# Sign bits in four matmul passes, V's maximum by DMA, shared idle matmuls and a new order in a fused attention and MoE kernel

## The chip, the core and the metric

The kernel runs on one core of a Trainium2 chip. The metric is the device time of one execution in microseconds (us), lower is better. The core has a matrix engine (TensorE, PE in the profile, with its weight loads as PEld), a vector engine (VectorE, DVE), a scalar engine (ScalarE, ACT), GpSimd (POOL), and SyncE (SP), which here issues every DMA. Each engine runs its own instructions in the order in which they were issued and waits for the others by semaphores. PE writes to PSUM; DVE and ACT read PSUM and SBUF; POOL reads SBUF.

## What is computed

Attention in which a query sees only the keys of its own hash bucket, and behind it a layer that mixes tokens and channels. There are 4 batches, 8 heads, 768 tokens, 64 channels per head and 6 hash bits.

```python
q_bits = (np.einsum('bhsd,dk->bhsk', q, proj) > 0).astype(np.int64)
k_bits = (np.einsum('bhsd,dk->bhsk', k, proj) > 0).astype(np.int64)
...
mask = q_bucket[:, :, :, None] == k_bucket[:, :, None, :]
scores = scale * np.matmul(q, k.transpose(0, 1, 3, 2))
scores = np.where(mask, scores, -1000000000.0)
scores = scores - np.max(scores, axis=-1, keepdims=True)
attn = np.exp(scores)
attn = attn / (np.sum(attn, axis=-1, keepdims=True) + 1e-09)
return np.matmul(attn, v).astype(np.float32)
...
theta = x @ w_theta
cos_t, sin_t = (np.cos(theta), np.sin(theta))
zr = x * cos_t
zi = x * sin_t
yr = np.einsum('ts,bsd->btd', w_tok_r, zr)
yi = np.einsum('ts,bsd->btd', w_tok_i, zi)
y = yr + yi
u = x + y
return (u + np.maximum(u @ w_ch, 0.0)).astype(np.float32)
```

## The kernel before

**Numbers in parts.** Single matmul passes carry fewer bits than fp32, so values are split into a high and a low part and multiplied in several passes. q and k are split by `high` (an ACT copy to a narrower fp32 form, line 643) and `low` (the remainder, line 646, on DVE or POOL) into the tile `hl`.

**Work by pairs of heads.** `prep_qk` and `prep_v` prepare two heads at once, 16 pairs in all. For the sign bits `bits` (line 660) multiplies `hl` by the projection's parts `pst` in two halves of 512 and 256 tokens, each into its own PSUM bank `pb`: three passes for q (high by high, high by low, low by high), three for k, accumulated into the same 64 rows. `sign` (line 668) compares those rows with 0 on DVE and writes `rows`. `first` (line 673) does the same for the very first head straight into qt and kt. `assemble` (line 710) copies `hl` and `rows` by DMA into the operands qt and kt of one head; three sets of these take turns (`SETS`).

**One head.** `maxima` (line 742) computes the scores `sq` once, in nine units, each reduced by DVE (`vmax`, line 768, tile `mc`), transposes the maxima on PE (`pmx`), makes a row of them and writes it into qt by DMA (`put`). `step` (line 812) then computes transposed scores `st`, now with the maximum subtracted in the matmul, exponentiates them on ACT (`pf`, line 846), and multiplies by V in `pv` (line 860), which accumulates `po`. A head has nine chunks of 128 by 512 (six in block 0, three in block 1), a pair 18. In a pair whose number is in `FULL` the fp32 `pf` is multiplied by the whole scaled V (`vw`). In the others `pf` becomes two fp16 parts, p1 (a copy, line 852) and p2 (the remainder, line 858), and three passes follow with V's two parts. `P1` and `P2` name the engines for these parts by step number.

**V's scale.** `prep_v` reduces the absolute maximum of V to one value per partition (`amax`, DVE, line 519), transposes it on PE into PSUM (`am_tr`), reduces it on DVE (`am_row`), multiplies it by ones on PE to bring it to all partitions (`am_all`), and copies it out (`am_out`, line 533). A power of two made of it scales V.

**MoE.** For every batch `moe` (line 915) transposes x in six token tiles (`pt_x`), multiplies by w_theta (`ps_th`), makes cosine and sine (`trig`), the products z in two fp16 parts, multiplies by the token weights (`py`, 36 passes a tile), adds, transposes again (`pt_u`), multiplies by w_ch (`ps_r`) and stores. The weights are prepared during the first pairs: token weights by `prep_wtok` (due times `W0`, `WS`), w_theta and w_ch by `split_weight` (`WTH`, `WC`).

**The order.** Nothing is issued where it is written. Each `op` has a name, a due time (`prio`, in steps; 96 steps in all, six to a pair), the engines it may run on with planned durations, the ops it waits for and the buffer slots it holds. `issue_all` (line 120) simulates the engines with those durations and issues for each engine, when it falls free, the available op with the earliest due time. The constants behind the function (`QK1`, `PV0`, `TH0`, `Y0`, `YS` and others) are those due times. If PE has nothing to do before `FILL`, it issues an idle matmul (`filler`, line 323), planned at 225 ns; each gets a new tile in a free bank of the PSUM pool `m`. That pool has four banks, the pools `mx` and `s` have two each.

Of the kernel before, what the change touches and what calls it, by code (L numbers as in the profile page):

```python
# [32 lines left out]
def lsh_attention_moe_kernel(ctx: ExitStack, tc: tile.TileContext, qk, wt, v, consts, w_theta, w_ch, out):  # L33
# [6 lines left out]
    P = 128  # L40
# [33 lines left out]
    psts = const.tile([P, 2, 2, 96], F32R, name="pst")  # L74
    POOL.memset(psts.bitcast(F32), 0.0)
    pst = {}
    for i, part in enumerate("hl"):
        flat = psts[:, i].rearrange("p a b -> p (a b)")
        pst["q", part], pst["k", part] = flat[:, :64], flat[:, 64:128]
# [12 lines left out]
    WAKE = {"ACT": 45, "DVE": 37, "PE": 58, "POOL": 105, "SP": 40}  # L92
    SHARED = {"qkl", "p1", "p2", "zf", "zh", "zl", "mag", "wlow", "whigh", "wmul", "wl", "vv2", "wtl"}
# [21 lines left out]
    FREE = dict(ft=2, mc=2, hl=1, rows=1, nat=2, wst=2, vv=2, x=2, z0=1, z1=1, xt=2, **BUFS)  # L115
# [3 lines left out]

    def issue_all():  # L120
        left = {}
        rng = random.Random(SEED)
        for i, o in enumerate(ops):
            o.key = (round(o.prio + JIT * rng.random(), 4), i)
            for sl in o.slots:
                left.setdefault(sl, []).append(o)
# [74 lines left out]
        used, seen, warm = {}, 0, False  # L201

# [119 lines left out]

    def filler(idx):
# [42 lines left out]
    def widened(srcs, n, nm, tag, prio, stage="x", by=1.0):  # L366
# [22 lines left out]
        a = op("wload", prio, on("SP", [(450, P * n * 8)] * m, load), slots=[sx, sz])  # L389
# [36 lines left out]
    def prep_wtok(n, prio):  # L426
# [26 lines left out]
        a = op("wload", prio, on("SP", [(450, P * S * 8)], load), slots=sl)  # L453
# [46 lines left out]
    vamax, vinv, vsc = (const.tile([P, B * NP], F32, name=nm) for nm in ("vamax", "vinv", "vsc"))  # L500
    zinv, zsc = (const.tile([P, B], F32, name=nm) for nm in ("zinv", "zsc"))
    vready = {b: [] for b in range(B)}

    def prep_v(b, hp, prio):
        t = {}
        sv, sm_, sa = Slot("vv"), Slot("m"), Slot("m")
# [14 lines left out]
        def am_tr():  # L521
            t["pa"] = bank(sa, [P, 2, P], f"pa_{b}_{hp}")
            PE.transpose(t["pa"][:1, 0], t["am"], ident)

        def am_row():
            t["a1"] = ap_.tile([1, 1], F32, tag="a1" + sa.tag, bufs=1, name=f"a1_{b}_{hp}")
            DVE.tensor_reduce(t["a1"], t["pa"][:1, 0], AX.X, ALU.max)

        def am_all():
            mm(t["pa"][:, 1, :2], t["a1"].to_broadcast([1, P]), ones1, True, True)  # L530

        def am_out():
            DVE.tensor_copy(vamax[:, col], t["pa"][:, 1, :1])
# [92 lines left out]
    def prep_qk(b, hp, G, g):  # L626
# [4 lines left out]
        for i in range(2):  # L631
            def half(i=i):
# [7 lines left out]
                def high():  # L640
                    if "hl" not in t:
                        t["hl"] = ap_.tile([P, 2, 2, S], F32R, tag=sh.tag, bufs=1, name=f"hl_{b}_{hp}")
                    ACT.activation(t["hl"][:, 0, i], u["nat"], AF.Copy)  # L643
# [3 lines left out]

                ld = op("qkload", G + QKL + 0.02 * i, on("SP", [(450, 2 * S * D * 4)], load), slots=[sn])
                hs.append(op("qkh", pr, on("ACT", 735, high), [ld], [sn, sh]))
# [5 lines left out]
        for lo, n_ in ((0, 512), (512, S - 512)):  # L655
            def signs(lo=lo, n_=n_):
# [580 lines left out]
```

## Time and profile before

| | us |
|---|---|
| median of 3 runs | 829.23 |
| lowest and highest | 828.43, 829.85 |
| profiled execution, its own time | 830.03 |
| span of its trace | 828.2 |
| DMA queue, share of 16 engines | 37.2% |

The profile shows one execution. Busy times are the time in which an engine had an instruction in flight. Matmuls are pipelined, so that one's own duration is longer than its distance to the next; the cost of a run of matmuls is read from the start of the next run. A view by groups lists line, engine, operation, output and inputs, count, busy us and mean ns of one, and then the idle time in front of them with what ended it. The chain of waits follows the work that ended last back from the end. A view by windows gives busy times in stretches, with the instruction count in brackets, and then the granted clock of PE, the share of the DMA engines and GB/s.

### The profile page before, as it was taken

What the parts mean: (1) busy time and instruction counts of PE and PEld (TensorE: products, weight loads), DVE (VectorE), ACT (ScalarE), POOL (GpSimd) and SP (SyncE); (2) the same over time, 40 slices, a digit from 0 to 9 for tenths busy, and PEclk for the clock granted to TensorE, in tenths of its full rate; (3) what the DMA queues carried; (4) which work ended last, traced back from release to release, by engine and by line L of the source; (5) the groups of instructions that cost most, each with busy time, mean ns of one, the idle gap of its engine ahead of it and who ended that gap; (6) DMA issues with size and microseconds to landing.
All of it is one profiled execution on the core that took longest, in us unless ns stands there. A gap on an engine that the chain in (4) does not pass through costs nothing.

```text
span 828.2 us, 17207 instructions
## 1 busy us (share of the span) xinstructions
PE 808.8 (98%) x6644; PEld 569.7 (69%) x6644; DVE 602.8 (73%) x1024; ACT 511.1 (62%) x871; POOL 372.9 (45%) x404
## 2 busy tenths in 40 slices
PE   8999999999999999999999999999999999999997
PEld 2588887676765667878667666678667666676554
DVE  5869989886896957797888766687988666357322
ACT  3366766785993635797987365467985554568100
POOL 2344444773676614684766342352685332113100
PEclk9999999999999999999999999999999999999999
DMA  8466759407016424544243434251333330000001
GB/s 231 99 201 189 223 151 240 123 11 168 18 44 156 121 60 122 127 87 108 69 96 85 112 94 110 57 141 33 93 81 82 76 74 14 15 27 1 13 26 38
DMA packets 33617, 79.00 MB, mean 95 GB/s; under 512 B 6360, under 2 KB 10648, under 8 KB 33536
## 3 DMA queue, kind: packets, MB, share of 16 engines
q1 hardware_dynamic: 33536, 77.91, 37.2%
q8 instruction: 52, 0.85, 0.4%
q14 instruction: 29, 0.24, 0.1%
HBM read 32.54 MB, written 6.29 MB: 47 GB/s over the span
## 4 chain that ended last, share of the span: by engine, by line
PE 87%; DVE 6%; ACT 4%; issue 1%; DMA 1%; SPq 1%; ACTq 0%; DVEq 0%
PE py L82 21%; PE po L82 15%; PE st L82 15%; PE ps_r L82 8%; PE sq L82 8%; PE ps_th L82 7%; PE fill L82 5%; PE pb L82 4%; DVE mc L768 2%; PE pt_u L957 1%; PE pt_x L957 1%; ACT pf L846 1%; PE pa L82 1%; ACT p L852 1%; DVE mc L777 1%
## 5 line engine op out<-in xcount | busy, mean ns | idle before, releaser
L846 ACT ACTIVATE pf<-st 128x512 f32<-128x512 f32 x288 | 167.8, 596 | 134.2 <-PE st L82 126.3
L858 POOL TENSOR_TENSOR p<-pf,p 128x512 f16<-128x512 f32 x135 | 167.5, 1252 | 182.7 <-ACT p L852 119.8
L768 DVE TENSOR_REDUCE mc<-sq 128x1 f32<-128x512 f32 (+1 forms) x288 | 191.5, 683 | 34.1 <-PE sq L82 32.4
L82 PE MATMUL py<-z,wtk 128*128 128x512 f16 x864 | 215.7, 381 | 0.0
L82 PE MATMUL st<-qt,kt 108*128 108x512 f32 (+3 forms) x768 | 195.8, 364 | 2.8 <-ACT pf L846 2.6
L852 ACT ACTIVATE p<-pf 128x512 f16<-128x512 f32 x234 | 140.7, 632 | 9.2 <-PE po L82 7.0
L82 PEld LDWEIGHTS st<-qt,kt 108*128 108x128 f32 (+1 forms) x768 | 119.1, 190 | 20.9 <-ACT pf L846 8.5
L82 PE MATMUL sq<-kt,qt 108*128 108x512 f32 (+1 forms) x384 | 128.9, 393 | 2.7 <-DVE mc L768 1.2
L82 PEld LDWEIGHTS <-wtk 128*128 128x128 f16 x864 | 72.4, 98 | 83.5 <-issue 18.3
L82 PEld LDWEIGHTS <-p 128*128 128x128 f16 x2808 | 106.8, 98 | 31.1 <-issue 14.0
L82 PE MATMUL po<-vv,p 128*128 128x65 f16 (+1 forms) x2808 | 124.5, 193 | 0.4 <-DVE p L858 0.4
L858 DVE TENSOR_TENSOR p<-pf,p 128x512 f16<-128x512 f32 x99 | 87.5, 888 | 35.0 <-ACT p L852 32.9
L82 PEld LDWEIGHTS sq<-kt,qt 108*128 108x128 f32 x384 | 66.7, 190 | 23.0 <-DVE mc L768 5.8
L1046 POOL TENSOR_TENSOR z<-f,z 128x512 f16<-128x512 f32 x34 | 46.4, 1370 | 59.6 <-ACT z L1040 40.3
L82 PE MATMUL ps_r<-wch,h_u 128*128 128x512 f32 x192 | 62.8, 408 | 0.7 <-ACT h_u L962 0.7
L82 PE MATMUL ps_th<-wth,h_x 128*128 128x512 f32 x192 | 62.0, 404 | 0.1
L789 POOL TENSOR_SCALAR fl<-row 6x128 f16<-6x128 f32 x32 | 28.4, 889 | 62.1 <-DVE row L785 44.7
L82 PEld LDWEIGHTS po<-vw,pf 128*128 128x128 f32 x432 | 54.5, 192 | 1.8 <-issue 0.2
L82 PE MATMUL po<-vw,pf 128*128 128x65 f32 x432 | 54.6, 274 | 0.0
L962 ACT ACTIVATE h_u<-pt_u 128x512 fp32r<-128x512 f32 x24 | 14.3, 597 | 64.0 <-PE pt_u L957 63.9
L82 PE MATMUL fill<-idle 128*128 128x512 f16 x121 | 48.0, 404 | 5.5 <-DVE ones L72 1.6
L646 POOL TENSOR_TENSOR hl<-nat,hl 128x768 fp32r<-128x768 f32 x24 | 48.1, 2013 | 10.6 <-ACT hl L643 10.5
(139 smaller groups left out, 1079.7 us busy)
## 6 DMA issues: line engine op xcount, KB each, us to landing
nat<-in_qk_dram SPq DMA_DIRECT2D x32, 384.0 KB
qt<-hl SPq DMA_DIRECT2D x31, 384.0 KB
kt<-hl SPq DMA_DIRECT2D x31, 384.0 KB
wst<-in_wt_dram SPq DMA_DIRECT2D x12, 768.0 KB
vb<-in_v_dram SPq DMA_DIRECT2D x16, 384.0 KB
out_dram<-x SPq DMA_DIRECT2D x24, 256.0 KB
qt<-hl SPq DMA_DIRECT2D x62, 96.0 KB
kt<-hl SPq DMA_DIRECT2D x62, 96.0 KB
```

The costliest lines, as they stand in the source:

```text
L82: PE.matmul(out_, l, r, start=start, stop=stop, skip_group_check=True)
L646: return lambda: eng.tensor_tensor(t["hl"][:, 1, i], u["nat"], t["hl"][:, 0, i].bitcast(F32), ALU.subtract)
L768: DVE.tensor_reduce(col()[:, cs], u["sq"], AX.X, ALU.max)
L777: DVE.tensor_tensor(t["mc"][:, :T], t["mc"][:, :T], t["mc"][:, T:], ALU.max)
L789: POOL.tensor_scalar(t["fl"], t["row"].bitcast(F32), -BIG / 4, PSC, ALU.is_lt, ALU.mult)
L846: ACT.activation(wide("pf", spf, F32), u["st"], AF.Exp, scale=1.0 / math.sqrt(D))
L852: ACT.activation(o_, u["pf"], AF.Copy)
L858: return lambda: eng.tensor_tensor(wide("p2", sp2, F16), u["pf"], u["p1"], ALU.subtract)
L957: PE.transpose(u["pt"][:, c], src()[:, c * P : (c + 1) * P], ident)
L962: ACT.activation(u["hi"], u["pt"], AF.Copy)
L1046: return lambda: eng.tensor_tensor(t["z"][r, 1][:, tt], u["f"], t["z"][r, 0][:, tt], ALU.subtract)
```

## The change

- **Sign bits.** The projection's high part lies in columns 0 to 63 of a 128-column operand, its remainder (now with the opposite sign) in columns 64 to 127. One pass of the high part of q gives both products, in PSUM rows 0 to 63 and 64 to 127; the low part needs one pass of 64 columns. So two passes for q and two for k. ACT copies rows 64 to 119 to SBUF (`total`), DVE subtracts them from rows 0 to 55 (`plus`), and `sign` compares in SBUF, on DVE or POOL.
- **V's maximum.** The transpose is a DMA of the 128 values into a row (`vrow`), the distribution a DMA of one value to 128 partitions. The PSUM bank that held the two products is not taken; the row is one buffer (`vr`).
- **Idle matmuls.** A filler writes again into the tile of the filler before, as long as that is the newest tile of its bank. Planned at 216 ns.
- **Order.** The planner counts extra time for a wide fp32 pass behind certain ops (`AFTER`, `WIDE`) and prefers, behind these, another op that is due up to `PEN` later. Tails by name count on PE alone. Some planned durations change. The projection may be split on POOL, and the constants are loaded behind the first q and k. In the first pair the high parts may be made on DVE.
- **Constants.** `FULL` loses pair 1. `P1` is ACT and `P2` POOL throughout. Nearly all due times are new.

```diff
-    psts = const.tile([P, 2, 2, 96], F32R, name="pst")
+    psts = const.tile([P, 2, 160], F32R, name="pst")
...
+    flat = psts.rearrange("p a b -> p (a b)")
+    pst = {"q": flat[:, :P], "k": flat[:, P : 2 * P]}
...
+    AFTER = {"pv": 84, "pv4": 30, "mtr": 40, "vall": 40, "xtr": 20}
+    WIDE = {"st", "qmax", "proj", "bits"}
...
+                    if best is not None and o.key[0] > best[0] + PEN:
+                        break
+                    if best is not None and o.name in WIDE:
+                        continue
                     if can(o):
-                        best, pick = o.key, o
-                        break
+                        best, pick = best or o.key, o
+                        if e != "PE" or o.name not in WIDE or before not in AFTER:
+                            break
...
-                lat = TAILS.get(o.name, TAIL_[e])
+                lat = TAILS.get(o.name, TAIL_[e]) if e == "PE" else TAIL_[e]
                 if e == "PE":
+                    if o.name in WIDE:
+                        dur += AFTER.get(before, 0)
+                    before = o.name
...
-        return op("fill", 0, on("PE", 225, lambda: mm(bank(sl, [P, 512], "fill"), idle_[:, :P], idle_, True, True)))
+        def go():
+            if sl.tag not in spare or spare[sl.tag] is not newest.get(sl.tag):
+                spare[sl.tag] = bank(sl, [P, 512], "fill")
+            mm(spare[sl.tag], idle_[:, :P], idle_, True, True)
+
+        return op("fill", 0, on("PE", 216, go))
...
+            h_, l_ = psts[:, :, : 2 * NM], psts[:, :, 64 : 64 + 2 * NM]
...
+            eng.tensor_tensor(l_, h_.bitcast(F32), pjs, ALU.subtract)
...
+    cload = op("consts", QKL + 0.03, on("SP", [(600, 0)], load_consts))
+    proj_ready = op("pst", PST, {"POOL": (1500, split_proj(POOL)), "DVE": (1100, split_proj(DVE))}, [cload])
...
         def am_tr():
-            t["pa"] = bank(sa, [P, 2, P], f"pa_{b}_{hp}")
-            PE.transpose(t["pa"][:1, 0], t["am"], ident)
+            dma(vrow, t["am"])
 
         def am_row():
-            t["a1"] = ap_.tile([1, 1], F32, tag="a1" + sa.tag, bufs=1, name=f"a1_{b}_{hp}")
-            DVE.tensor_reduce(t["a1"], t["pa"][:1, 0], AX.X, ALU.max)
+            DVE.tensor_reduce(vone, vrow, AX.X, ALU.max)
 
         def am_all():
-            mm(t["pa"][:, 1, :2], t["a1"].to_broadcast([1, P]), ones1, True, True)
-
-        def am_out():
-            DVE.tensor_copy(vamax[:, col], t["pa"][:, 1, :1])
+            dma(vamax[:, col], vone.to_broadcast([1, P]))
...
                 def bits():
                     u["pb"] = bank(sm_, [P, 512], f"pb_{b}_{hp}_{lo}")
-                    n = 0
-                    for i, nm in enumerate("qk"):
-                        for a_, c in (("h", 0), ("h", 1), ("l", 0)):
-                            mm(u["pb"][:64, :n_], pst[nm, a_], t["hl"][:, c, i, lo : lo + n_], n == 0, n == 5)
-                            n += 1
+                    cols = slice(lo, lo + n_)
+                    mm(u["pb"][:, :n_], pst["q"], t["hl"][:, 0, 0, cols], True, False)
+                    mm(u["pb"][:, :n_], pst["k"], t["hl"][:, 0, 1, cols], False, False)
+                    mm(u["pb"][:64, :n_], pst["q"][:, :64], t["hl"][:, 1, 0, cols], False, False)
+                    mm(u["pb"][:64, :n_], pst["k"][:, :64], t["hl"][:, 1, 1, cols], False, True)
...
+                    ACT.activation(u["r"].bitcast(F32), u["pb"][64:120, :n_], AF.Copy)
+
+                def plus():
+                    DVE.tensor_tensor(u["r"].bitcast(F32), u["pb"][:56, :n_], u["r"].bitcast(F32), ALU.subtract)
+
+                def sign(eng):
+                    return lambda: eng.tensor_scalar(u["r"], u["r"].bitcast(F32), affs[:56, 0:1], affs[:56, 1:2], ALU.is_ge, ALU.mult)
...
-FULL = [0, 1, 2]
+FULL = [0, 2]
...
-P1 = [[0, 12, ['ACT', 'DVE']], [12, 999, ['ACT']]]
-P2 = [[0, 999, ['POOL', 'DVE']]]
+P1 = [[0, 999, ['ACT']]]
+P2 = [[0, 999, ['POOL']]]
...
-Y0_3 = 16.204
-YS_3 = 7.658
-Y1_3 = 3.219
+Y0_3 = 32.886
+YS_3 = 18.321
+Y1_3 = 0.085
...
-QK1 = -5.44
-PV0 = -4.578
-W0 = 2.347
-WS = 1.758
+PEN = 0.282
+QK1 = -3.942
+PV0 = -4.358
+W0 = 1.598
+WS = 2.439
```

More of the change, by code (lines that the diff above doesn't have):

```diff
@@ L201, in issue_all @@
         used, seen, warm = {}, 0, False
+        before = None
         def pace(t, dur, part):
@@ L452, in prep_wtok @@
         sl = [sw_]
[L453 removed]
+        a = op("wload", prio, on("SP", [(350, P * S * 8)], load), slots=sl)
         b_ = op("wlow", prio, on("DVE", 80 + 400, low), [a], sl)
@@ L500, in lsh_attention_moe_kernel @@
     vamax, vinv, vsc = (const.tile([P, B * NP], F32, name=nm) for nm in ("vamax", "vinv", "vsc"))
+    vrow = const.tile([1, P], F32, name="vrow")
+    vone = const.tile([1, 1], F32, name="vone")
     zinv, zsc = (const.tile([P, B], F32, name=nm) for nm in ("zinv", "zsc"))
@@ L638, in load, with high, go @@
                     dma(u["nat"], qk[b, hp, :, i])
[L640 to L643, printed above, removed]
+                def high(e):
+                    def go():
+                        if "hl" not in t:
+                            t["hl"] = ap_.tile([P, 2, 2, S], F32R, tag=sh.tag, bufs=1, name=f"hl_{b}_{hp}")
+                        if e == "ACT":
+                            ACT.activation(t["hl"][:, 0, i], u["nat"], AF.Copy)
+                        else:
+                            DVE.tensor_copy(t["hl"][:, 0, i], u["nat"])
+                    return go
                 def low(eng):
                     return lambda: eng.tensor_tensor(t["hl"][:, 1, i], u["nat"], t["hl"][:, 0, i].bitcast(F32), ALU.subtract)
-                ld = op("qkload", G + QKL + 0.02 * i, on("SP", [(450, 2 * S * D * 4)], load), slots=[sn])
-                hs.append(op("qkh", pr, on("ACT", 735, high), [ld], [sn, sh]))
+                ld = op("qkload", G + QKL + 0.02 * i, on("SP", [(330, 2 * S * D * 4)], load), slots=[sn])
+                hs.append(op("qkh", pr, {"ACT": (735, high("ACT")), "DVE": (475, high("DVE"))} if g == 0 else on("ACT", 735, high("ACT")), [ld], [sn, sh]))
                 ls.append(op("qkl", pr, {"DVE": (870, low(DVE)), "POOL": (1750, low(POOL))}, [hs[-1]], [sn, sh]))
@@ L675, in first @@
                         DVE.tensor_scalar(
-                            dst[MR : MR + NM, 0, lo : lo + n_], u["pb"][r0 : r0 + NM, :n_], affs[r0 : r0 + NM, 0:1], affs[r0 : r0 + NM, 1:2], ALU.is_ge, ALU.mult
+                            dst[MR : MR + NM, 0, lo : lo + n_], u["r"].bitcast(F32)[r0 : r0 + NM], affs[r0 : r0 + NM, 0:1], affs[r0 : r0 + NM, 1:2], ALU.is_ge, ALU.mult
                         )
-                b1 = op("bits", G + at("QK1", b), on("PE", 10 + 1388 * n_ / 512, bits), hs + ls + [proj_ready], [sm_, sh])
+                pr1 = G + at("QK1", b)
+                b1 = op("bits", pr1, on("PE", 10 + 925 * n_ / 512, bits), hs + ls + [proj_ready], [sm_, sh])
+                b1 = op("btot", pr1, on("ACT", 60 + 420 * n_ / 512, total), [b1], [sm_, sr])
+                b1 = op("bplus", pr1, on("DVE", 70 + 540 * n_ / 512, plus), [b1], [sm_, sr])
+                rest = []
                 if g == 0:
-                    t.setdefault("direct", []).append(op("sign0", G + at("QK1", b) - 0.01, on("DVE", 2 * (230 + 560 * n_ / 512), first), [b1], [sm_]))
-                fs.append(op("sign", G + at("QK1", b), on("DVE", 190 + 540 * n_ / 512, sign), [b1], [sm_, sr]))
+                    rest = [op("sign0", pr1 - 0.01, on("DVE", 2 * (70 + 280 * n_ / 512), first), [b1], [sr])]
+                    t.setdefault("direct", []).extend(rest)
+                fs.append(op("sign", pr1, {"DVE": (65 + 272 * n_ / 512, sign(DVE)), "POOL": (90 + 1030 * n_ / 512, sign(POOL))}, [b1] + rest, [sr]))
             signs()
@@ L1132 @@
 WIN = {"m": 3, "tmp": 3}
-MX0 = -4.222
-MX1 = 0.485
+MX0 = -3.92
+MX1 = 0.367
 PIECES = [{1: (0, 3)}, {0: (0, 2), 1: (2, 3)}]
-PF = 0.229
-KA = 1.914
-KB = 1.297
-KV = 0.471
-KN = 2.21
-AB = -1.043
-WTH = 17.154
-WTS = -3.096
-WC = 28.626
-WCS = 1.32
-P1 = [[0, 12, ['ACT', 'DVE']], [12, 999, ['ACT']]]
-P2 = [[0, 999, ['POOL', 'DVE']]]
+PF = 0.656
+KA = 2.074
+KB = 1.097
+KV = 0.9
+KN = 1.554
+AB = -1.588
+WTH = 17.112
+WTS = 0.063
+WC = 25.356
+WCS = 4.365
+P1 = [[0, 999, ['ACT']]]
+P2 = [[0, 999, ['POOL']]]
 GR = 2
-GR1 = 2
+GR1 = 0
 GROUPS = [[(0, 3), (3, 6)], [(0, 4), (4, 6)], [(0, 2), (2, 4), (4, 6)]]
-JIT = 0
-SEED = 162248
-TH0_3 = 4.023
-TH1_3 = 0.304
-Y0_3 = 16.204
-YS_3 = 7.658
-Y1_3 = 3.219
-MX0_0 = -2.545
-MX1_0 = -0.458
-AS0_0 = -5.127
-PV0_0 = -3.986
-QK0_0 = -2.659
-QK1_0 = -8.282
-HOLD = 0.312
-FILL = 190000
-TH0_0 = 0.49
-TH1_0 = 0.849
-Y0_0 = 10.381
-Y1_0 = 1.107
-YS_0 = 5.176
-AHEAD = 1.931
-QKL = -8.066
-QK0 = -3.777
-QK1 = -5.44
-AS0 = -1.124
-PV0 = -4.578
-LV0 = -3.999
-W0 = 2.347
-WS = 1.758
-TH0 = 0.512
-TH1 = 0.818
-Y0 = 10.167
-YS = 6.472
-Y1 = 2.716
+TH0_3 = 4.252
+TH1_3 = 0.07
+Y0_3 = 32.886
+YS_3 = 18.321
+Y1_3 = 0.085
+MX0_0 = -2.536
+MX1_0 = 0.04
+AS0_0 = -4.728
+PV0_0 = -6.631
+QK0_0 = -6.273
+QK1_0 = -10.464
+HOLD = 0.177
+FILL = 190000
+TH0_0 = 0.566
+TH1_0 = 0.25
+Y0_0 = 10.85
+Y1_0 = 2.254
+YS_0 = 8.488
+PEN = 0.282
+AHEAD = 1.948
+PST = -12.621
+QKL = -8.174
+QK0 = -2.283
+QK1 = -3.942
+AS0 = -4.062
+PV0 = -4.358
+LV0 = -3.808
+W0 = 1.598
+WS = 2.439
+TH0 = 1.365
+TH1 = 0.38
+Y0 = 9.202
+YS = 6.317
+Y1 = 2.708
 _INS = ["v", "moe_w_theta", "moe_w_ch"]
```

53 lines of the change are left out of this document (26 added, 27 removed).

## The prediction

> **What bounds the kernel now.** I read the page first: busy times, then the shares of the chain of work that ended last.
>
> ```profile
> PE 808.8 (98%) x6644; PEld 569.7 (69%) x6644; DVE 602.8 (73%) x1024; ACT 511.1 (62%) x871; POOL 372.9 (45%) x404
> PE 87%; DVE 6%; ACT 4%; issue 1%; DMA 1%; SPq 1%; ACTq 0%; DVEq 0%
> PE py L82 21%; PE po L82 15%; PE st L82 15%; PE ps_r L82 8%; PE sq L82 8%; PE ps_th L82 7%; PE fill L82 5%; PE pb L82 4%; DVE mc L768 2%; PE pt_u L957 1%; PE pt_x L957 1%; ACT pf L846 1%; PE pa L82 1%; ACT p L852 1%; DVE mc L777 1%
> ```
>
> PE is busy 98% of the span and 87% of the chain, so a pass taken from PE should come off the end. But 5% of the chain is `fill`, the idle matmul that computes nothing: there PE was waiting for others. Next I asked for engine busy times by stage, and then the same for the fills alone (first number the length, then PE busy; in the first fence PEld, DVE, ACT and POOL follow, in brackets the instructions).
>
> ```profile
> 33.00:66.00 33.00, 32.78 (x227) 27.52 (x226) 25.23 (x49) 19.68 (x34) 13.53 (x16) 1.00 0.74 206
> 66.00:101.00 35.00, 34.22 (x253) 30.11 (x252) 32.31 (x64) 24.64 (x42) 16.72 (x17) 1.00 0.71 197
> 142.00:166.00 24.00, 23.20 (x212) 14.94 (x212) 21.22 (x44) 19.17 (x37) 17.16 (x20) 1.00 0.52 129
> 166.00:187.00 21.00, 20.16 (x228) 14.74 (x225) 18.27 (x32) 17.52 (x31) 16.02 (x14) 1.00 0.07 21
> ```
> ```profile
> 0.00:33.00 33.00, 23.33 (x56) 1.00 0.55 158
> 33.00:142.00 109.00, 6.70 (x18) 1.00 0.73 200
> 142.00:187.00 45.00, 12.46 (x33) 1.00 0.31 78
> 187.00:220.00 33.00, 5.53 (x15) 1.00 0.46 102
> ```
>
> So there are three regimes. Up to 33 us PE waits for the first head. From 33 to 142 us, where pairs 0 to 2 multiply whole fp32 weights (`FULL`), and after 220 us, PE is the bound. From 142 to 187 us, with split fp16 weights and no MoE matmuls yet, fills take 12.46 of 45 us: there DVE, ACT and POOL set the pace.
>
> **The change, part by part.** The sum is made against the profiled execution, 830.0 us for a span of 828.2; the median of the three runs, 829.2, lies 0.8 below it.
>
> *Sign bits.* The timeline of PE gives each run's start, so its cost is the next start less its own.
>
> ```profile
> 306.31 1.58 PE L82 MATMUL pb<-hl,pst 128*64 128x512 f32 x6
> 307.72 0.63 PE L82 MATMUL ps_r<-wch,h_u 128*128 128x512 f32 x2
> 310.52 0.86 PE L82 MATMUL pb<-hl,pst 128*64 128x256 f32 x6
> 311.23 0.54 PE L82 MATMUL po<-vv,p 128*128 128x65 f16 x12
> 311.61 0.63 PE L957 MATMUL pt_u<-ident,x 128*128 128x128 f32 x4
> 312.47 1.20 PE L82 MATMUL st<-qt,kt 108*128 108x256 f32 x6
> 313.60 0.38 PE L82 MATMUL pa<-ones,a 1*128 1x2 f32 x2
> 313.90 0.73 PE L82 MATMUL ps_r<-wch,h_u 128*128 128x512 f32 x2
> ```
>
> Six 512-column passes take 1.41 us (0.235 each), six of 256 columns 0.71 (0.118 each): 2.12 us a pair. Four of each take 1.41. Fifteen pairs behind the first: 15 x 0.71 = **10.6 us less**. Two of the four passes now load 128 weight columns instead of 64. The groups of weight loads, and a run of 256-column scores that loads 128 columns for each pass:
>
> ```profile
> L82 PEld LDWEIGHTS pb<-hl,pst 128*64 128x64 f32 x192 | 25.3, 140 | 11.5 <-issue 1.2 <-ACT qt L693 0.6 <-DVE x L1074 0.3
> L82 PEld LDWEIGHTS st<-qt,kt 108*128 108x128 f32 (+1 forms) x768 | 119.1, 190 | 20.9 <-ACT pf L846 8.5 <-issue 0.2
> 169.24 0.63 PE L82 MATMUL st<-qt,kt 108*128 108x256 f32 x4
> 169.71 0.54 PE L82 MATMUL po<-vv,p 128*128 128x65 f16 x12
> ```
>
> The wide load shows 190 ns against 140, but four passes with it start within 0.47 us, 0.118 each: nothing shows, and I add nothing. The Trainium skill ("TensorE: Matmul & The Clock Gate", LDWEIGHTS) says that a weight load's time goes with its columns alone, which the 140 and 190 ns follow in direction. If its extra 50 ns were not hidden on the four wide loads of a pair, 16 pairs would give back 3.2 us; the row at 169.24 speaks against it, and the sum goes without.
>
> The result is now two halves to be subtracted: an ACT copy from PSUM, a DVE subtraction, and a comparison that reads SBUF, on DVE or POOL.
>
> ```profile
> L671 DVE TENSOR_SCALAR rows<-pb,cst 56x512 fp32r<-56x512 f32 (+1 forms) x32 | 20.8, 665 | 7.7 <-PE pb L82 7.7
> L852 ACT ACTIVATE p<-pf 128x512 f16<-128x512 f32 x234 | 140.7, 632 | 9.2 <-PE po L82 7.0
> L858 POOL TENSOR_TENSOR p<-pf,p 128x512 f16<-128x512 f32 x135 | 167.5, 1252 | 182.7 <-ACT p L852 119.8
> L858 DVE TENSOR_TENSOR p<-pf,p 128x512 f16<-128x512 f32 x99 | 87.5, 888 | 35.0 <-ACT p L852 32.9
> L646 POOL TENSOR_TENSOR hl<-nat,hl 128x768 fp32r<-128x768 f32 x24 | 48.1, 2013 | 10.6 <-ACT hl L643 10.5
> ```
>
> By these, 32 halves add at most 32 x 0.63 = 20 us to ACT (511 busy), and to DVE nothing or about what L671 takes, 21 us. Their cover is that a pair's bits are due some 4 steps ahead of their use (`QK1`). Without it each half would be late by an ACT and a DVE step, about 1.3 us: 0 taken, +20 us (15 pairs) the far end.
>
> *V's maximum.* The two `ones` passes take 0.30 us (313.60 to 313.90), the transpose before them 0.03 to 0.1: 15 x 0.35 = **5.2 us less**. In exchange 32 DMAs of 512 bytes are queued on SP. The nearest priced transfer is the row of maxima (with the score that waits for it):
>
> ```profile
> 29.42 0.71 SPq L792 DMA_DIRECT2D qt<-row  x1
> 33.22 0.63 PE L82 MATMUL st<-qt,kt 108*128 108x512 f32 x2
> ```
>
> Each holds SP for about 0.7 us, 22 us in all, and lands within 3.8 us. SP now waits for DVE's `am` and `vone`; behind it stand the assembly of qt and kt and the stores. DVE waits at `vone` for a landing, and `vmax`, which frees PE's score banks, stands behind it. V is asked for 4 steps ahead (`PV0`), over 25 us, as 96 steps take some 700 us, so I take 0; 16 x 2 waits of 0.3 us would be +10, the far end. Freeing one `m` bank of PSUM can help by as little.
>
> *FULL without pair 1.* Its 18 chunks take 8 fp32 records each now, and would take 12 fp16 passes. The fp32 chunk stands in the chain in order of time:
>
> ```profile
> 45.02 0.84 PE po L82 x8
> ```
>
> 0.84 less 0.38 (311.23 to 311.61) is 0.46; x 18 = **8.3 us less** on PE in a stage that PE bounds. It adds 18 x 0.63 = 11 us to ACT and 18 x 1.25 = 23 us to POOL there. Pair 1 ran from 66 to 101 us, where ACT is busy 24.6 and POOL 16.7 of 35: with it they come to 36 and 39, over the stage. They fit only with what lies beside it: 33 to 66 us has 13 us of ACT and 19 of POOL idle, and the preparation of the token weights, which uses both, is spread out (`WS` 1.76 to 2.44). With 0 and 2 whole and 1 and 3 split, PE-heavy and POOL-heavy pairs alternate, so I count the gain in full and keep the doubt for the rivals.
>
> *P1, P2.* All narrow copies go to ACT, all remainders to POOL. The 99 on DVE become 99 x 1.25 = 124 us of POOL; with pair 1 it has about 373 + 124 + 23 = 520 us: under the end, but see the second rival. DVE loses 88 us, where it was the fullest next to PE (21.2 of 24 us).
>
> *Idle matmuls and the start.*
>
> ```profile
> 6.66 0.96 DVE L646 TENSOR_TENSOR hl<-nat,hl 128x768 fp32r<-128x768 f32 x1 [0.21 <-ACT hl L643]
> 9.36 4.11 PE L82 MATMUL pb<-hl,pst 128*64 128x512 f32 x12
> 13.42 4.26 PE L82 MATMUL fill<-idle 128*128 128x512 f16 x10
> 17.41 0.75 PE L82 MATMUL sq<-kt,qt 108*128 108x256 f32 x3
> ```
>
> Ten fills take 4.0 us, 0.40 each, since each takes a new tile in the same bank and waits for the one before. The planner counts 225 ns. So fills run late: the first bits are ready to start at 7.62 and start at 9.36, and the bits themselves need 4.06 us, against 2.12 later, though the granted clock is 1.00. With one shared tile nothing waits, fills fall to at most a pass (0.235), bits can start near 7.9 and take 1.4 to 2.7. The longer sign chain gives back about 1.3, the fills before 17.41 no longer overhang by 2. I take **5 us less**, between 0 and 9. The Trainium skill (the same page, Part 1) has a clock gate that opens after about 3.4 us of sustained work; the halved rate here agrees, and denser fills would open it before the bits. Without that, the bits would gain about 1.3 us less.
>
> *Fills behind 33 us.* 66 fills stand for 6.70 + 12.46 + 5.53 = 24.7 us. Half goes if they cost half, more if DVE's relief feeds PE, less where POOL is late: I take **8 us less**, between 20 less and 15 more.
>
> *Order.* The planner now knows 84 ns for a wide pass behind `pv` and puts another one there. Two runs of scores, behind `po` and behind `sq`:
>
> ```profile
> 422.23 0.70 PE L82 MATMUL st<-qt,kt 108*128 108x512 f32 x2
> 422.78 0.55 PE L82 MATMUL po<-vv,p 128*128 128x65 f16 x12
> 427.26 0.63 PE L82 MATMUL st<-qt,kt 108*128 108x512 f32 x2
> 427.73 0.87 PE L82 MATMUL pb<-hl,pst 128*64 128x256 f32 x6
> ```
>
> 0.55 against 0.47: 0.08 a place. There are 234 split chunks (L852); avoiding it behind one in six is **3 us less** (0 to 10). For the last batch y runs across tokens: 0 to 4 less at the tail, where I take **1**, and 6 more if PSUM banks run out.
>
> Sum: 10.6 + 5.2 + 8.3 + 5 + 8 + 3 + 1 = 41; 830.0 - 41 = 789; I say **790**.
>
> **Rivals.** *Freed passes become waiting* (0.17). The bits' and V's passes are gone, but pair 1, short of ACT and POOL, and the order only raise starvation before 220 us: 830 - 10.6 - 5.2 - 5 = 809, with the waits of the new DMAs up to 819. For it: 142 to 187 us, where PE already starved. Against: DVE loses work there.
>
> *POOL takes over* (0.07, the other side). A split pair asks of POOL 18 x 1.25 = 22.5 for remainders, 2 x 2.01 for the low halves, and about 6 for flags, sums and signs: 32 to 33 us, when split pairs came 21 to 24 us apart (142, 166, 187). If pairs 1, 3, 4 and 5 are paced so, 4 x 11 = 44 us come on: 830 - 41 + 8 + 44 = 841. It decides where POOL's share in 60 to 190 us passes 90%. Against it: low halves and signs may go to DVE, and a whole pair beside it lets POOL catch up.
>
> *The order finds more* (0.09). All fills behind 33 us but a few go, ten more at start and switches: 830 - 41 - 17 = 772, down to 762.
>
> **Numbers.** The forecast holds 0.67, from 775 to 805. To leave out no more than 0.2 I reach to 772 and 814. The measurement tells 0.2% (1.7 us) from no change; only a narrow strip between the first rival and the second lies there: faster 0.90, same 0.03, slower 0.07.
>
> **What would show it.** Right: 128 `pb` matmuls instead of 192, near 1.41 us a pair; no `pa` from V; `po<-vw` 288 instead of 432; the first scores before 30 us; fills about the planner's 216 ns apart; p2 on POOL alone with POOL under 85% in each stage. Wrong: more fill time between 33 and 220 us than 24.7; DVE waiting for DMA at `vone` in microseconds; SP's waits for `am` ahead of late qt; POOL full in 60 to 190 us. I would be off most where the order decides: the 8 us of fills and the 5 of the start.

## The result, and the profile after

The changed kernel takes 809.72 us (median of 4, 807.68 to 810.32) against 828.83 us (828.19 to 829.85) for the kernel before, measured together: a ratio of 0.976 (95% interval 0.974 to 0.978), 19 us less. The forecast was 790, 39 us less; about half of it came. Now and then an execution of a kernel ran a per cent or more longer at a lower granted clock; one of b1 (826.66 us) did so and is left out of its median below.

The page of the changed kernel (its profiled execution took 809.67 us): the span, PE's busy time, the granted clock in 40 slices, the shares of the chain of waits by engine and by line, and POOL's largest group.

```profile
span 807.8 us, 17469 instructions
...
PE 788.5 (98%) x6655; PEld 567.3 (70%) x6655; DVE 545.3 (68%) x950; ACT 529.8 (66%) x914; POOL 490.3 (61%) x519
...
PEclk9969998699999999999999999999999999999999
...
PE 77%; ACT 9%; DVE 7%; DMA 4%; issue 2%; POOL 1%; SPq 0%; ACTq 0%; DVEq 0%; POOLq 0%
PE py L82 21%; PE po L82 15%; PE st L82 15%; PE ps_r L82 8%; PE sq L82 7%; PE ps_th L82 4%; DVE mc L808 2%; PE pb L82 2%; ACT pf L886 2%; PE fill L82 2%; PE pt_u L997 1%; DMA vrow<-vam 1%; DMA vb<-in_v_dram 1%; ACT L886 1%; ACT z L1063 1%
...
L898 POOL TENSOR_TENSOR p<-pf,p 128x512 f16<-128x512 f32 x252 | 306.9, 1236 | 105.7 <-ACT p L892 53.6
```

PE is as full as before, 98%, but its part of the chain fell from 87% to 77%: ACT, DVE and now DMAs (4%, V's row among them) stand in it. And in the clock row two slices show 6 and one 8, where before every slice showed 9. These slices lie ahead of the y matmuls. The timeline of PE gives the first of them and PE's last row, before and then after:

```profile
220.48 2.12 PE L82 MATMUL py<-z,wtk 128*128 128x512 f16 x9
...
824.13 0.40 PE L82 MATMUL ps_r<-wch,l_u 128*128 128x512 f32 x1
```
```profile
215.34 1.47 PE L82 MATMUL py<-z,wtk 128*128 128x512 f16 x6
...
803.63 0.40 PE L82 MATMUL ps_r<-wch,l_u 128*128 128x512 f32 x1
```

So the first part became 5.1 us shorter (220.48 to 215.34), the second 15.4 (603.65 to 588.29). In the second, ten pairs have their bits and V's maximum (six lie ahead of it): 10 x (0.71 + 0.35) = 10.6 us by the prediction's prices, and 4 for order and tail, 14.6 in all. That part came as forecast. Of the 26 us left for the first part, 21 are missing.

Busy times of PE, PEld, DVE, ACT and POOL in three stretches of the first part, for the changed kernel, and then the fills alone in the prediction's four windows:

```profile
33.00:66.00 33.00, 29.70 (x157) 24.32 (x157) 22.42 (x49) 18.40 (x30) 12.70 (x18) 0.79 0.67 182
66.00:101.00 35.00, 35.00 (x314) 27.55 (x314) 30.12 (x53) 28.60 (x52) 31.58 (x28) 1.00 0.69 179
...
142.00:187.00 45.00, 43.20 (x385) 32.81 (x384) 31.97 (x69) 33.95 (x60) 36.21 (x36) 0.87 0.40 90
```
```profile
0.00:33.00 33.00, 23.35 (x82) 1.00 0.67 189
33.00:142.00 109.00, 17.27 (x63) 0.90 0.69 186
142.00:187.00 45.00, 7.91 (x28) 0.87 0.40 90
187.00:220.00 33.00, 0.00 (x0) 1.00 0.49 110
```

The fills were to shrink. From 33 to 220 us they are 25.2 us against 24.7 before, only earlier: 17.27 against 6.70 in 33 to 142 us, where PE had been the bound. Half of these lie where pair 1 now runs with split weights. The fills of that window, before and then after, and POOL's longest run of work in the changed kernel:

```profile
66.00:101.00 35.00, 1.56 (x4) 1.00 0.71 197
```
```profile
66.00:101.00 35.00, 9.16 (x33) 1.00 0.69 179
```
```profile
84.36 13.29 POOL L898 TENSOR_TENSOR p<-pf,p 128x512 f16<-128x512 f32 x10
```

While POOL makes these ten remainders one behind the other, PE runs 20 of the 33 idle matmuls. In 33 to 66 us PE does less than before (29.70 busy against 32.78) at a granted clock of 0.79. Finer windows, and PE's timeline there (the bracket is idle time and what ended it):

```profile
45.00:48.00 3.00, 1.81 (x12) 1.38 (x12) 0.75 (x2) 1.77 (x4) 1.69 (x3) 1.00 1.02 416
48.00:51.00 3.00, 1.97 (x7) 1.03 (x6) 2.90 (x6) 2.32 (x4) 0.12 (x1) 0.54 1.01 329
51.00:54.00 3.00, 3.00 (x15) 2.90 (x15) 2.93 (x8) 0.52 (x2) 1.73 (x1) 0.50 1.06 214
54.00:57.00 3.00, 3.00 (x16) 3.00 (x16) 1.52 (x2) 2.61 (x5) 0.00 (x0) 0.50 1.04 203
...
138.00:150.00 12.00, 12.00 (x53) 11.42 (x52) 4.68 (x15) 6.41 (x11) 6.51 (x8) 0.50 0.77 201
```
```profile
44.13 0.74 PE L82 MATMUL st<-qt,kt 108*128 108x512 f32 x2 [0.96 <-ACT pf L886]
...
46.90 0.41 PE L82 MATMUL pm<-vb,ones 128*33 128x128 f32 x2 [1.19 <-POOL vb L581]
...
50.39 1.39 PE L82 MATMUL sq<-kt,qt 108*128 108x256 f32 x3 [1.03 <-DVE mc L808]
...
54.21 4.51 PE L82 MATMUL po<-vw,pf 128*128 128x65 f32 x20
58.48 1.20 PE L82 MATMUL sq<-kt,qt 108*128 108x512 f32 x3
```

PE waits three times for about a microsecond with no idle matmul between. The clock halves and stays at 0.50 from 51 to 57 us although PE is busy throughout; 20 passes of `po` take 4.3 us (54.21 to 58.48), 0.21 each, against 0.105 (0.84 / 8) in the prediction's chunk. It happens again from 138 to 150 us. DVE's timeline shows what was late:

```profile
42.09 0.15 DVE L388 TENSOR_SCALAR vinv<-vamax 128x1 f32<-128x1 f32 x1 [2.76 <-DMA vamax<-vone]
...
47.22 0.56 DVE L467 TENSOR_SCALAR wst<-wst 128x768 uint32<-128x768 uint32 x1 [2.57 <-DMA wst<-in_wt_dram]
```

The first is the new DMA of V's maximum, the second a late load of token weights; before, DVE never waited for such a load. Behind each on DVE stand things that PE needs.

### The profile page after: what moved, and what is told of

Same layout as the page of the kernel before. It is cut to its first block, busy times and chain, and to the rows that moved or that the text cites. A ratio compares the mean times of both kernels' runs of the same rounds, so it can differ in the third digit from the quotient of the medians.

```text
span 807.8 us, 17469 instructions
## 1 busy us (share of the span) xinstructions
PE 788.5 (98%) x6655; PEld 567.3 (70%) x6655; DVE 545.3 (68%) x950; ACT 529.8 (66%) x914; POOL 490.3 (61%) x519
## 4 chain that ended last, share of the span: by engine, by line
PE 77%; ACT 9%; DVE 7%; DMA 4%; issue 2%; POOL 1%; SPq 0%; ACTq 0%; DVEq 0%; POOLq 0%
PE py L82 21%; PE po L82 15%; PE st L82 15%; PE ps_r L82 8%; PE sq L82 7%; PE ps_th L82 4%; DVE mc L808 2%; PE pb L82 2%; ACT pf L886 2%; PE fill L82 2%; PE pt_u L997 1%; DMA vrow<-vam 1%; DMA vb<-in_v_dram 1%; ACT L886 1%; ACT z L1063 1%
## 5 line engine op out<-in xcount | busy, mean ns | idle before, releaser
L898 POOL TENSOR_TENSOR p<-pf,p 128x512 f16<-128x512 f32 x252 | 306.9, 1236 | 105.7 <-ACT p L892 53.6
L808 DVE TENSOR_REDUCE mc<-sq 128x1 f32<-128x512 f32 (+1 forms) x288 | 189.3, 683 | 39.5 <-PE sq L82 38.4
L892 ACT ACTIVATE p<-pf 128x512 f16<-128x512 f32 x252 | 150.4, 627 | 20.0 <-PE po L82 18.0
L82 PEld LDWEIGHTS <-p 128*128 128x128 f16 x3024 | 112.9, 98 | 34.2 <-issue 17.1
L82 PE MATMUL po<-vv,p 128*128 128x65 f16 x3024 | 130.0, 193 | 2.0 <-POOL p L898 1.7
L82 PEld LDWEIGHTS <-wtk 128*128 128x128 f16 x864 | 72.0, 98 | 77.0 <-issue 15.4
L82 PE MATMUL sq<-kt,qt 108*128 108x256 f32 (+1 forms) x384 | 122.2, 388 | 2.8 <-DVE mc L808 2.2
L1075 DVE SCALAR_TENSOR_TENSOR f<-x,zr,z 128x512 f32<-128x512 f32 x48 | 45.4, 965 | 10.6 <-ACT z L1063 7.7
L82 PEld LDWEIGHTS po<-vw,pf 128*128 128x128 f32 x288 | 44.6, 233 | 1.1
L82 PE MATMUL po<-vw,pf 128*128 128x65 f32 x288 | 44.6, 316 | 0.0
L1121 DVE SCALAR_TENSOR_TENSOR x<-ps_r,x 128x512 f32<-128x512 f32 x24 | 16.5, 688 | 39.2 <-PE ps_r L82 39.2
L82 PEld LDWEIGHTS ps_th<-wth,h_x 128*128 128x128 f32 x192 | 35.3, 188 | 8.6 <-issue 0.4
```

Source lines behind the costliest of these rows:

```text
L82: PE.matmul(out_, l, r, start=start, stop=stop, skip_group_check=True)
L808: DVE.tensor_reduce(col()[:, cs], u["sq"], AX.X, ALU.max)
L892: ACT.activation(o_, u["pf"], AF.Copy)
L898: return lambda: eng.tensor_tensor(wide("p2", sp2, F16), u["pf"], u["p1"], ALU.subtract)
L1075: DVE.scalar_tensor_tensor(u["f"], tl[b][:, tt], t["zr"][:, 2 * tt + r : 2 * tt + r + 1], t["zw"][r][:, tt], ALU.mult, ALU.mult)
L1121: DVE.scalar_tensor_tensor(tl[b][:, to], r_["ps"], 0.0, tl[b][:, to], ALU.max, ALU.add)
```

## The experiments

Each kernel was run in turn with the kernel before; the medians are compared with 829 for before and 809.7 for after.

| run | us, median (range) | ratio to before (95%) |
|---|---|---|
| before with shared tile (b1) | 815.33 (813.62–816.03) | 0.982 (0.970–0.993) |
| after with own tiles (a2) | 828.97 (826.49–831.78) | 1.000 (0.996–1.003) |
| before, no late fills (b2) | 824.81 (823.38–834.75) | 0.995 (0.991–0.999) |
| before, shared tile, no late fills (b8) | 817.03 (816.49–817.34) | 0.985 (0.984–0.987) |
| before with four-pass bits (b4) | 837.64 (836.41–841.94) | 1.012 (1.009–1.015) |
| before with V's maximum by DMA (b5) | 888.77 (881.83–896.83) | 1.064 (1.062–1.067) |
| after with two passes more (a3) | 815.14 (813.08–816.13) | 0.982 (0.974–0.989) |
| after with six-pass bits (a9) | 816.48 (815.52–816.72) | 0.985 (0.983–0.986) |
| after without V's exchange (a4) | 806.26 (805.77–807.69) | 0.973 (0.972–0.975) |
| after, pair 1 weighed down (a15) | 813.14 (811.08–815.05) | 0.981 (0.979–0.983) |
| after, kept warm (a1) | 803.81 (803.30–807.32) | 0.969 (0.962–0.977) |
| after, warm, loads behind maxima (a16) | 807.33 (806.05–809.05) | 0.974 (0.972–0.976) |

**The shared tile.** Alone in the old order (b1), and taken out of the new one (a2).

```diff
-        return op("fill", 0, on("PE", 225, lambda: mm(bank(sl, [P, 512], "fill"), idle_[:, :P], idle_, True, True)))
+        def go():
+            if sl.tag not in spare or spare[sl.tag] is not newest.get(sl.tag):
+                spare[sl.tag] = bank(sl, [P, 512], "fill")
+            mm(spare[sl.tag], idle_[:, :P], idle_, True, True)
+
+        return op("fill", 0, on("PE", 225, go))
```

> The kernel before, with the shared tile for idle matmuls as its only edit; the order is the same. Theory of the prediction: the first bits start near 7.9 us and run at the full rate, the first scores come 3 to 6 us earlier, and the fills from 142 to 220 us cost half; 5 to 12 us faster than before, 817 to 824. Rival: the fills stand in waits for other engines and take nothing from the end: within 2 us of 829.

> The changed kernel, with every idle matmul in a new tile again; the order is the same. Theory of the prediction: the shared tile is worth 5 us at the start and half of the fills behind it, so this is 5 to 12 us slower than 809.7. Rival: fills only stand where PE waits anyway, so that it is within 2 us; the first bits then start as late as in the kernel before (9.4 us) but the end does not move. The clock may also differ, since fills that wait for each other keep PE less busy: if the start stays at half rate, the first scores come 1 to 3 us later.

It is worth 13.7 us alone and 19.3 us in the new order, more than either theory gave. Without it all the rest of the change gains nothing (828.97): in a2's trace the first y matmuls start at 238.11, 17.6 us later than before, and the part behind them is 16.4 us shorter (587.24). PE's timeline of b1 at the start, and its first y matmuls:

```profile
5.75 1.05 PE L85 MATMUL pb<-hl,pst 128*64 128x512 f32 x3
...
9.76 2.32 PE L85 MATMUL fill<-idle 128*128 128x512 f16 x10
...
205.91 2.12 PE L85 MATMUL py<-z,wtk 128*128 128x512 f16 x9
```

Ten fills take 2.3 us where before ten took 4.0, the bits start at 5.75 instead of 9.36, and the y matmuls 14.6 us earlier than before: 9.4 us earlier than in the changed kernel, which has less to do up to there. From there to the end b1 takes as long as before (603.55 us). In a2 the 23 fills ahead of the first bits last from 1.56 to 15.77 us.

**The late fills.** All that the planner puts behind 33 us left out, in the old order with own tiles (b2) and with the shared tile (b8).

```diff
-                fn()
+                if o.name != "fill" or now < 33000:
+                    fn()
```

> The kernel before, in its own order, without the idle matmuls that its planner puts behind 33 us (those of the first 33 us stay). Theory (the idle matmuls are what holds the clock in the gaps of the first 220 us): the granted clock halves in further stretches between 33 and 220 us, and the time grows by 10 us or more, 839 us or above. Rival (behind 33 us the idle matmuls, each with a tile of its own, only fill or delay): the clock row stays as before and the time is 821 to 830 us.

> The kernel before in its own order with the idle matmuls in shared tiles, as in the run of the shared tile alone (815.7 us), and without those that the planner puts behind 33 us. Theory (each with a tile of its own waits for the one ahead of it and costs about what the clock gains, so leaving them out gave 4 us; with shared tiles they cost little and hold the clock): without them the granted clock falls in places between 40 and 200 us and the time is 3 to 8 us above the shared tile alone, 819 to 824 us. Rival (they are of no use in either form): 812 to 816 us with the clock at full in all slices.

Both theories miss. With own tiles the late fills cost 4.1 us, within the range of b2's rival; shared, they are worth 1.7 us (817.03 against 815.33), less than b8's theory. The fall of the clock that b8's theory expected did come: two slices of its clock row show 8. b2's profiled execution took 834.75 us, ten above its median, so its trace isn't used. What sharing gives beside them, 824.81 - 817.03 = 7.8 us, must lie in the fills of the first 33 us, which both kept.

**The bits.** Alone in the old order (b4); in the new order two throwaway passes added per half (a3), or the six-pass form put back with copy, subtraction and second comparison gone (a9). The expectations count eleven pairs behind the first y matmuls; the traces show ten.

```diff
-                            mm(u["pb"][:64, :n_], pst[nm, a_], t["hl"][:, c, i, lo : lo + n_], n == 0, n == 5)
...
+                    mm(u["pb"][:64, :n_], pst["k"][:, :64], t["hl"][:, 1, 1, cols], False, True)
...
+                    ACT.activation(r.bitcast(F32), u["pb"][64:120, :n_], AF.Copy)
+                    DVE.tensor_tensor(r.bitcast(F32), u["pb"][:56, :n_], r.bitcast(F32), ALU.subtract)
```
```diff
+                    for _ in range(2):
+                        mm(u["pb"][:64, :n_], pst["q"][:, :64], t["hl"][:, 0, 0, cols], True, False)
```

> The kernel before, in its own order, with one part of the change alone: the sign bits in four passes with the remainder in spare columns, and the ACT copy and the DVE subtraction that add the two halves up, issued at the place of the comparison. Theory, from the traces before and after (behind the first y matmuls at about 215 us the freed time came off one for one, ahead of them it turned into idle matmuls and waits): the eleven pairs whose bits lie behind 215 us give 11 x 0.71 = 7.8 us and the early ones nothing, so 821 us (819 to 823) against 829. Rival, as the prediction had it: all fifteen pairs of halves give 10.6 us, so 818.5 us. Second rival: the copy and the subtraction hold ACT and DVE longer than the passes gave, 827 to 831 us.

> The changed kernel with two throwaway passes of 64 columns ahead of the four passes of the sign bits in each half, so that six run again; the result is overwritten, nothing else changes, and the order is the same. If PE passes come off the end one for one, as the prediction counted, this is 9 to 12 us slower than 809.7 (16 pairs times 0.71 us = 11.3). Rival: part of them lies in waits of PE before 190 us; then it is 5 to 9 us slower.

> The changed kernel in its own order with the sign bits back in six passes of 64 columns and one comparison from PSUM: the ACT copy, the DVE subtraction and the second comparison are gone. It measures what the four-pass form is worth inside the new order, copy and subtraction included. Theory (behind 215 us passes count one for one, before it they are covered; the sums lie beside a busy PE): eleven pairs give 11 x 0.71 = 7.8 us, so 817.5 us (816 to 819) against 809.7, and the first y matmuls stand where they stood, within 2 us. Rival, the prediction's sum: fifteen pairs, 10.6 us, so 820.3 us, the first y matmuls 2.8 us later. Second rival: the sums cost in the first 215 us about what the passes give there and more, so that the time is 812 to 815 us and the first y matmuls come 3 us or more earlier.

In the old order the better form loses 8.7 us. The waits of DVE in b4 (total, times, longest) hold a new entry:

```profile
DVE rows L673 <- ACT rows L672: 17.1, 20, 2.3
```

DVE stands at the head of its queue until ACT has copied, with the maxima behind it. In the new order the form gains: a9 is 6.8 us slower, 5.7 behind the first y matmuls (588.3 to 594.0) and 1.0 before them (216.30); a3 gives 5.4 for the passes alone, 5.7 behind the first y matmuls and 0.8 before them in its trace. But a9 has a handicap of its own: there V's row shares a tile (`shared`) with the projection, whose split on POOL waits for the first row:

```profile
11.14 0.29 POOL L376 TENSOR_TENSOR shared<-cst 128x48 f32<-128x48 f32 x1 [5.84 <-DMA shared<-vam]
```

So copy and subtraction show no cost there (6.8 is not below 5.4), but a small one may be hidden by that late start.

**V's maximum.** By two DMAs in the old order (b5); in the new order without the exchange (a4).

```diff
-            PE.transpose(t["pa"][:1, 0], t["am"], ident)
+            dma(vrow, t["am"])
...
-            mm(t["pa"][:, 1, :2], t["a1"].to_broadcast([1, P]), ones1, True, True)
+            dma(vamax[:, col], vone.to_broadcast([1, P]))
```
```diff
-            dma(vrow, t["am"])
+            pass
...
-            DVE.tensor_reduce(vone, vrow, AX.X, ALU.max)
+            DVE.tensor_copy(vamax[:, col], t["am"])
...
-            dma(vamax[:, col], vone.to_broadcast([1, P]))
+            pass
```

> The kernel before, in its own order, with one part of the change alone: V's maximum over the partitions by two small DMAs in place of a transpose and a matmul on PE. Theory: eleven pairs behind 215 us give 0.35 each, 3.9 us, so 825 us (824 to 827). Rival: each of the two DMAs takes about 2 us from issue to landing and SP, which issues in order, waits for the maximum and for the row before it can issue the loads behind them, so that loads come late: 829 us or more, with waits of SP for vam and vone and of others for DMAs in the trace.

> The changed kernel without the two DMAs that carry V's maximum from partition to partition: each partition scales V by its own maximum, so the maximum over the partitions is left out of the computation. The DVE reduction over the row is replaced by a copy of one column. Theory (the DMAs' waits, 20.8 us of SP for the maximum and 11.6 us of DVE, lie mostly beside a busy PE): at most 2 us faster than after, 808 to 810 us. Rival (they are what turns the freed passes of the first 215 us into gaps): 4 to 7 us faster, 803 to 806 us, and the stretch of idle matmuls from 33 to 190 us shrinks.

In an order that doesn't know of the DMAs they cost 60 us. DVE's waits in b5 (where `shared` holds V's row too), and below them the same two in the changed kernel:

```profile
DVE vone L528 <- DMA shared<-vam: 43.0, 15, 4.7
...
DVE vinv L364 <- DMA vamax<-vone: 27.0, 16, 2.4
```
```profile
DVE vinv L388 <- DMA vamax<-vone: 6.8, 6, 2.8
DVE vone L553 <- DMA vrow<-vam: 4.8, 5, 1.6
```

70 us of DVE's waiting became 11.6 by the new order. What is left of the exchange still costs 3.5 us (a4, between the two theories), 2.9 of them before the first y matmuls (212.41).

**Pair 1.** Does PE's time matter where pair 1 runs? Two more idle matmuls ahead of the PE operation that follows each of its 18 chunks (a15).

```diff
+                if e == "PE":
+                    for _ in range(EXTRA.get(npe, 0)):
+                        if free["m"]:
+                            filler(free["m"][-1]).alts["PE"][1]()
+                    npe += 1
                 fn()
```

> The changed kernel in its own order, with two more idle matmuls behind each of the 18 chunks of probabilities times V of pair 1: 36 x 0.216 = 7.8 us of PE, nearly what the change freed there by taking pair 1 out of the float32 path (8.3 us). Theory (between 30 and 215 us PE doesn't set the pace, so what the change freed there went into idle matmuls and waits): the time moves by less than 3 us, 807 to 812 us. Rival (PE sets the pace there, and the freed 8.3 us were a gain that something else took back): 816 us or more.

3.4 us of 7.8 came back: between the theories, nearer to the first. But the granted clock changed with it (a mean of 0.985 in a15's profiled execution against 0.978): in PE's timeline `po` and `st` ahead of the first y matmuls take 3.8 us less than in the changed kernel. So it isn't shown that the rest is covered by waiting.

**The halved clock.** 38 more idle matmuls (the expectation says 35) at ten places around 44 to 60 and 133 to 150 us, by the same edit with other counts (a1); the same, and the first DVE and ACT operations on a token-weight load issued behind the two maxima that follow them, near 47 and 140 us (a16).

```diff
-                fn()
+                if o.prio in late and o.name in ("wlow", "whigh", "wsign", "wabs"):
+                    late[o.prio][1].append(fn)
+                else:
+                    fn()
```

> The changed kernel with 35 more idle matmuls at ten fixed places of PE's order between 41 and 150 us, in or beside the waits of PE; the order of all other work and every computed value stay as they are. Theory: what is missing from the forecast went into two stretches (48 to 62 us and 134 to 154 us) in which the granted clock of the changed kernel is 0.5, some 33 us in all, because PE stood in short waits without idle matmuls and then ran fp32 passes of 65 columns. With the waits filled the clock stays at 1.00 and 10 to 16 us come off: 794 to 800 us. Rival: PE was waiting for DVE and ACT there, so that the clock does not matter; then the time stays within 2 us of 809.7, though the clock is 1.00.

> The changed kernel with the 38 more idle matmuls of the warm run (803.8 us), and with the DVE operations on the late token-weight loads put behind the maxima that follow them, at two places: near 47 us (DVE sat 2.6 us idle for the load with two maxima behind it) and near 140 us (2.1 us). Theory (what remains of the gaps is DVE's wait for these loads at the head of its queue): PE's waits for the maxima there shrink, the first y matmuls come 1 to 4 us earlier than in the warm run and the time is 800 to 803 us. Rival (PE waits there for other things too, or the idle matmuls already cover it): 803 to 806 us, no better than the warm run.

The clock row of a1 is whole again:

```profile
PEclk9999999999999999999999999999999999999999
```

The time falls by 5.9 us, and the first y matmuls come 5.8 us earlier (209.53): more than the rival's 2, far less than the theory's 10 to 16. Ahead of them PE's work takes 12.7 us less, each run counted from its start to the next, 9.0 of it in `po`; the idle matmuls take 8.3 more and the waits 1.3 less. The theory had the price of the halved clock right and left out the price of the idle matmuls. (a1's trace is of its slowest execution, 807.32 us; its part behind the first y matmuls is 3.5 us longer than in the changed kernel.) a16 adds nothing (2.4 us below after). DVE's timeline in a1 and in a16 shows one reason:

```profile
46.38 0.56 DVE L473 TENSOR_SCALAR wst<-wst 128x768 uint32<-128x768 uint32 x1 [2.48 <-DMA wst<-in_wt_dram]
...
48.80 1.29 DVE L814 TENSOR_REDUCE mc<-sq 128x1 f32<-128x512 f32 x2
```
```profile
47.26 0.35 DVE L631 SCALAR_TENSOR_TENSOR mt<-pm,vsc,mh 1x128 f16<-1x128 f32 x1 [3.37 <-ACT mt L628]
...
48.10 1.29 DVE L826 TENSOR_REDUCE mc<-sq 128x1 f32<-128x512 f32 x2
```

With the load out of the way DVE waits for `mt`, which hangs on V's late scale through POOL and `pm`; the maxima come 0.7 us earlier, no more. One late input had hidden another. In a16 the granted clock also fell again (0.82 and 0.50 in 57 to 60 and 60 to 63 us, 0.68 and 0.75 between 150 and 156), so its time doesn't tell what the moved loads alone are worth. a1 is the fastest kernel of the study, though its range (803.3 to 807.3) overlaps that of a16; by its executions the halved clock is priced at 2 to 6 us, the added idle matmuls included.

## Why the prediction came out half right

**Right: where PE is the bound.** Behind the first y matmuls passes came off nearly one for one. In PE's timeline of the changed kernel the four passes of a pair are

```profile
540.96 1.18 PE L82 MATMUL pb<-hl,pst 128*128 128x512 f32 x4
541.97 0.63 PE L82 MATMUL st<-qt,kt 108*128 108x512 f32 x2
...
543.38 0.64 PE L82 MATMUL pb<-hl,pst 128*128 128x256 f32 x4
543.86 0.39 PE L82 MATMUL sq<-kt,qt 108*128 108x512 f32 x1
```

1.01 + 0.48 = 1.49 us against 1.41 forecast: the wide weight load costs little or nothing. Over the ten pairs there, each run counted from its start to the next, `pb` takes 6.7 us less than before (7.1 forecast), and the 3.8 us of `pa` are gone (3.5 forecast). The second part of the run is 15.4 us shorter; the forecast, with order and tail counted there, makes it 14.6.

**Half right: POOL.** The 841 us of the second rival did not come, and POOL is at 80% in 142 to 187 us. But in 66 to 101 us it reaches 31.58 of 35 us (90%), above the 85% that the prediction named as a sign of being right. PE's waits for its remainders, 1.7 us in all, don't clear it: where PE would wait, the planner puts idle matmuls, and they stand beside POOL's ten remainders in a row. What a faster POOL would give there was not tried.

**Wrong: that the gains add up ahead of 220 us.** The step that failed is "33 to 142 us ... PE is the bound" for the kernel after the change, and with it counting pair 1, the early pairs and the saving on fills in full there. Term by term:

| step of the prediction | forecast | what the runs showed |
|---|---|---|
| sign bits | 10.6 less | 5.4 (a3) to 6.8 (a9): 5.7 behind the first y matmuls, about 1 of 3.5 before |
| V's maximum | 5.2 less, DMAs 0 | on PE 3.8 behind; the DMAs' waits cost 3.5 (a4) |
| FULL without pair 1 | 8.3 less | not isolated: `po` ahead of the first y matmuls takes 1.7 less, and 10.7 less where the clock holds (a1) |
| start 5 and fills 8 (the shared tile) | 13 less | 13.7 alone (b1), 19.3 in the new order (a2) |
| order 3, tail 1 | 4 less | about 5 behind the first y matmuls (15.4 - 6.7 - 3.8); ahead of them not a term of its own (b4, b5) |
| the clock stays at full | 0 | two stretches at half the clock, 2 to 6 more (a1) |

These sizes come from different orders and can't be added. What the traces give exactly is where PE's time ahead of the first y matmuls went (us, each run counted from its start to the next):

| | before | b1 | after | a1 |
|---|---|---|---|---|
| all work but fills | 176.1 | 173.9 | 169.0 | 156.3 |
| fills | 39.5 | 24.4 | 36.5 | 44.7 |
| waits | 4.9 | 7.6 | 9.8 | 8.5 |
| start of the first y matmuls | 220.5 | 205.9 | 215.3 | 209.5 |

The forecast took about 14 us off the work here (five pairs' bits and maxima, and pair 1) and 13 off the fills. The halved clock left 7 of the 14, and with the clock held (a1) the work is 20 us less. The fills fell by 15 us in the old order, but by 3 in the new one, where waits grew by 5: PE's freed time became waiting.

The shared tile's size was right in the old order: 7.8 us in the first 33 us (forecast 5) and 13.7 - 7.8 = 5.9 behind (forecast 8). But the change gave part of the start back: of the 7.7 us by which b1's first `st` is earlier (33.22 to 25.48) the changed kernel keeps 3.1 (30.07). Its first bits start later, behind constants loaded behind V, q and k and split on POOL; POOL's timeline and then PE's:

```profile
8.37 0.29 POOL L374 TENSOR_TENSOR pst<-pst,pjs 128x48 fp32r<-128x48 f32 x1
```
```profile
9.16 1.76 PE L82 MATMUL pb<-hl,pst 128*128 128x512 f32 x8
```

b1's bits are under way at 5.75, but through only at 9.65, those of the changed kernel at 10.76, and the first scores follow at 12.99 and 14.86. So the late constants stand for at most about 1 of the 4.6 us that are lost, and V's exchange for another (without it, a4, the first `st` starts at 29.12). Most of the rest comes between the first scores and the first `st`; its cause stays open. Yet a9, whose first `st` is 4.4 us later still, has its y matmuls only 1.0 us later: between 30 and 215 us the kernel catches up with what it loses, and loses what it gains.

The first rival, *freed passes become waiting*, told 809 us and its place: "pair 1 ... and the order only raise starvation before 220 us". That is what happened, through DVE's late inputs and the clock, and in 66 to 101 us beside a full POOL. That its 809 meets the measured 809.7 is luck: it takes bits and maxima in full and 5 us for the shared tile, which gave 13.7. It should have had more weight: fills already stood for 24.7 us of that stage, which says that PE there is not what decides.

The *order* was mis-sized in kind. It was priced as 3 us of switches; but without it the two other parts lose 8.7 and 60 us. It is the condition under which an ACT copy in front of DVE, or a DMA in front of both, costs little.

What stays open: how much pair 1 alone is worth (a15 weighs PE down and moves the clock, but leaves ACT's and POOL's added work in place), what a relieved POOL would give, what the new order would give without the other parts, and whether an order planned with the true clock would end the gaps.

## What to carry to other kernels

Where idle matmuls stand in a stage, PE isn't its bound, however full its row is: price freed passes there at a part, and nearly one for one only where no filler runs. An operation moved from PE to an engine with a wait in front is priced with the queue behind it; the same V exchange cost 60 us in an order that ignored it and 3.5 in one that knew it. Look at what fillers write: one that takes a new tile waits for the last one, and sharing the tile was worth 13.7 us alone and 19 in the new order. Idle matmuls that hold the clock have a price too: in a1 8.3 us of them bought 12.7.

## What the runs showed of the hardware

The granted clock fell after waits of 0.96 and 1.19 us with PE busy 1.8 of 3 us, not after one long wait, and stayed at 0.50 through 51 to 57 us and 138 to 150 us with PE busy in all of it, on 65-column fp32 passes among others. The Trainium skill ("TensorE: Matmul & The Clock Gate", Part 1) has the clock open after about 3.4 us of sustained work and drop after an idle window of that length; neither is what these rows show. Thirty-eight idle matmuls, 8 us of added work, made the kernel 5.9 us faster.
